# Attention and a gated feed-forward layer in one kernel: weight sums moved into the last pair of chunks, other banks, another static order

## The chip, the cores and the metric

The kernel runs on one core of a Trainium2 chip. The metric is the device time of one launch in microseconds, the median of the runs shown. Matrix products run on TensorE (PE), elementwise work on VectorE (DVE), ScalarE (ACT) and GpSimd (POOL); nearly all transfers are issued by SyncE (SP).

## The reference

```python
# attention: batch 8, heads 8, 576 tokens, head size 64; causal
scores = matmul(q, k.T) / 8
mask_local   = (rel >= 0) & (rel < 32)                 # heads 0 to 3
mask_strided = (rel >= 0) & (pos_q % 32 == pos_k % 32) # heads 4 to 7
attn = softmax(where(mask, scores, -1e9))
x = matmul(attn, v)          # as [4608 tokens, 512]
# feed-forward
xn = x / sqrt(mean(x * x) + 1e-6) * rms_g
g = xn @ w_gate              # 512 -> 1536
out = (g * sigmoid(g) * (xn @ w_val)) @ w_out   # 1536 -> 512
```

## The kernel before

**Precision.** Every large product is made of three passes. An operand x is split into a rounded high half (a cast) and a low half (a subtraction), both in the format that PE streams at full rate, and high x high, low x high and high x low are added in PSUM. So each operand costs a cast and a subtraction on ACT, DVE or POOL, and each 128x512 block of a product is three matmuls.

**Tiling.** Attention is cut into 96 units (`wus`, L434): batch b, pair of heads p, part j of three. Heads 0 to 3 (p = 0, 1) work on bands of tokens, heads 4 to 7 (p = 2, 3) on residues. Each unit runs `step_s` (scores on PE into the PSUM tile `pair`, maximum, exponential, norm; the split of q and k is `split`, L499), `step_t` (transposes, on DVE for most units) and `step_o` (values on PE, copied into `raw`). The result is cut into 9 chunks of 512 tokens, three `raw` tiles in turn. Chunks 0 to 6 (`NCL` = 7) pass through the feed-forward part one by one, while the attention of later chunks is made beside them; chunks 7 and 8 are done together at the end.

**A chunk of the loop.** It has 12 slots u, one per 128 columns of the 1536. `slot_g` and `slot_v` make gate and value into the banks `g` and `v` (L952), DVE and ACT form the product h (tanh on ACT, the steps at L967 and L978), `slot_h` splits it and `slot_o` adds it into the four output banks `a0` to `a3` (L1006). The output weight of a slot comes from a ring of `RING` = 4 buffers (`or0` to `or3`), filled from DRAM by `stream`. `rms` makes the next chunk's root: squares summed over the head pairs (`square`), a total over the partitions on PE, a root on ACT, one reciprocal over 128x512 on DVE (L896) and four scalings of `raw` (L900).

**The last pair.** `pair_of_chunks` (L1106) treats chunks 7 and 8 and the weights of gate and value as matrices of two by two blocks, so that seven products do for eight: A11, S1, A12, S2, S4, S3, A22. For each u, `quad(u)` (L1272) makes the seven, each six matmuls (L1283), into three banks p, q, r, and combines them on ACT and DVE; even and odd u have different banks. Four of the seven read sums of weights. `transform_gv` makes them for each u in the main loop: `joined` (L1052) adds the halves of gate and value, `minus` (L1056) forms the differences, `finish_set` splits them (L1070, L1076) and stores them in DRAM (`twg`); the pair fetches them back, two sets at a time. The sums on the other side, of the chunks, are made at its start in the buffers `ssq` and `srt` (L1212), which also hold output blocks on their way to DRAM. A second layer (`oproduct`, L1426) makes the output in seven products again, from sums of the output weight that `transform_o` has put into DRAM.

**PSUM.** There are eight banks. `g` and `v` are tiles of their own; `b0` and `b1` are the halves of the tile `pair`, `a0` and `a1` of `acc01`, `a2` and `a3` of `acc23`. The quads use (`g`, `v`, `b0`) and (`b1`, `a0`, `a1`) in turn.

**What sets the order.** Each operation is recorded by `Plan.op` with an engine (or several to choose from), a cost, the keys that it reads and writes, and whether it needs the SBUF port that DVE and POOL are taken to share. `Plan.order` computes due times from the end backwards (`series`, `latest`) and lays out a static order for each engine (`forward`): among the operations that could start within a hold time, the one due first. Two sets of parameters, `PASS_A` and `PASS_B`, hold before and after the point `SWITCH`. The order is then fixed; each engine runs its list in turn and waits where an operand isn't there.

Of the kernel before, what the change touches and what calls it, by code (L numbers as in the profile page):

```python
# [10 lines left out]
F32 = mybir.dt.float32  # L11
# [12 lines left out]
P = 128  # L24
# [5 lines left out]
NX = 3  # L30
RING = 4
# [22 lines left out]
PRE = 13  # L54
CD = 1.0
CA = 1.0
CP = 1.0
LATC = 150.0
EAT = 2000.0
PM = 15  # L60
# [83 lines left out]
class Plan:  # L144
# [15 lines left out]
    def op(self, eng, cost, at, fn, reads=(), writes=(), bytes_=0, rel=0.0, lock=(), tab=None, port=False, chain=False, also=None):  # L160
        i = len(self.ops)
        deps = set()
# [22 lines left out]

    def order(self):
# [12 lines left out]
    def series(self, users, hold, chf, dmt, rounds):  # L199
# [3 lines left out]
        for i in range(n - 1, -1, -1):  # L203
            ways, _, nb, _, _, _, chain = ops[i]
            eng = min(ways, key=lambda e: ways[e][0])
            own = ways[eng][0] + (dmt if nb else self.TAIL[eng])
            t = max([-due[u] + (0.0 if eng in ops[u][0] else self.LAT) for u in users[i]], default=0.0) + own
# [8 lines left out]
    def latest(self, users, took, length):  # L216
# [7 lines left out]
        for _ in range(n):  # L224
# [12 lines left out]
            for d in ops[i][1]:  # L237
                t = start[i] + (0.0 if on[d] == e and not ops[d][2] else self.LAT) + long[d] - ops[d][0][on[d]][0]
# [6 lines left out]
    def forward(self, users, due, hold, due2=None, hold2=None):  # L245
# [6 lines left out]
        def enter(i):  # L252
            ways, deps, _, rel, _, _, _ = ops[i]
            ready[i] = {e: max([end[d] + (0.0 if on[d] == e and not ops[d][2] else self.LAT) for d in deps] + [rel]) for e in ways}
# [24 lines left out]
        while len(out) < n:  # L279
            best = None  # L280
            for e, lst in avail.items():
                cand = []
                for i in lst:
# [6 lines left out]
                    cand.append((s, due[i], i))  # L290
# [38 lines left out]
def attn_moe(ctx: ExitStack, tc: tile.TileContext, qT: bass.AP, kT: bass.AP, vl: bass.AP, vs: bass.AP,  # L329
# [57 lines left out]
    tt = [sbt([P, 2 * CH], n) for n in ("tt", "th0")]  # L387

# [45 lines left out]
    wus = [(b, p, j) for b in range(NB) for p in range(NH // 2) for j in range(3)]  # L434
# [5 lines left out]
    for i in range(n_pro - TLAG, last + 1):  # L440
# [43 lines left out]
    for u in range(RING):  # L484
        wraw["o", u] = sb.tile([P, 1024], U32, name=f"or{u}")

    def wkey(key):
        return ("or", key[1] % RING) if key[0] == "o" else ("w", key)

    def wtag(key):  # L490
        return f"or{key[1] % RING}" if key[0] == "o" else f"w{key[0]}{key[1]}"
# [254 lines left out]
    def step_o(units):  # L746
# [23 lines left out]
        for x, (i, vt, m, n, tl, pT, po) in enumerate(todo):  # L770
# [27 lines left out]
            def evac(e, moves=moves):  # L798
# [6 lines left out]
               writes=[("raw", c % NX, p) for c in cs] + ["free2"] * (i == 11), also=way("e", ("DVE", dve(nt * m) + 80 * (len(moves) - 1), False)))  # L805


    def square(c, p, at):
# [15 lines left out]
        else:  # L824
            dk = "srt" if p else "ssq"
# [7 lines left out]
            if p:  # L833
# [3 lines left out]
    def rms(c, bk, at):  # L837
# [58 lines left out]
        op("DVE", 3270, at, lambda: nc.vector.reciprocal(out=roots["srt"], in_=roots["srt"]), writes=["srt"])  # L896
# [100 lines left out]
    def slot_o(c, u, at):  # L997
        h = 0
        if c and u == 2 * (c - 1):
            transform_o(c - 1)  # L1000
        for t in (0, 2, 1, 3):
            def fn(t=t):
                sl = slice(t * P, t * P + P)
                wt = W[("o", u)]
# [3 lines left out]
            op("PE", 681, at + t, fn, reads=[("hh", h), ("hl", h), wkey(("o", u))], writes=[("S", t // 2 + 1), ("T", t // 2 + 1), f"a{t}"] if u == 0 and c == 0 else [f"a{t}"], chain=True)  # L1008
# [20 lines left out]
    twg = [dp.tile([P, 2048], F32, name=f"tg{u}") for u in range(NU)]  # L1029
# [3 lines left out]
    def tset(i, w):  # L1033
        if (i, w) not in TS:
            TS[i, w] = sb.tile([P, 2 * CH], F32R, name=f"{'tl' if w else 'th'}{i}")
        return TS[i, w]

    def tkeys_of(i):
        return [("ts", i, w) for w in range(2)]
# [11 lines left out]
    def joined(key, dst, dk):  # L1051
        elementwise(CH, lambda e: both(e).tensor_tensor(out=dst, in0=W[key][:, 0].bitcast(F32), in1=W[key][:, 1].bitcast(F32), op=ALU.add),  # L1052
                    [wkey(key)], [dk])

    def minus(width, dst, a, b, keys):
        elementwise(width, lambda e: both(e).tensor_tensor(out=dst, in0=a, in1=b, op=ALU.subtract), [], keys)  # L1056

    turn_ = [0]

    def finish_set(dram, dk):  # L1060
        i = 0
        more = [("zo", 0), ("zo", 1)] if not turn_[0] else []
# [687 lines left out]
```

## Time and profile before

| | |
|---|---|
| time, median of 3 runs | 1041.87 us (1041.74 to 1043.63) |
| the profiled execution's own time | 1042.75 us |
| its span, first to last instruction | 1041.0 us |
| granted PE clock, mean | 0.990 |
| DMA traffic | 146.28 MB, mean 141 GB/s |

The page divides the span into 40 slices; a digit is the busy share in tenths:

```profile
PE   8899998999999999999999999999999989999998
...
DVE  4799999988789887887889998889996775455781
...
POOL 6224656763367653765236633356533510001300
PEclk9899999999999999999999999999999989999999
```

Attention and loading fill the first part, the main loop runs to about 840 us (slice 32), the pair of chunks from there to the end. POOL has almost nothing to do in the last eight slices. A row of a group of instructions gives line, engine, operation, result and operands, shape and count, then the busy time and the mean of one, then the engine's idle time ahead of them and who ended it.

### The profile page before, as it was taken

The numbers are of one execution on the slowest core, as the hardware profiler recorded it, in microseconds if no ns is written. First come the engines' busy times: TensorE is split into PE (matmuls) and PEld (weight loads), VectorE is DVE, ScalarE is ACT, GpSimd is POOL, SyncE is SP. The second block draws the span as 40 slices with busy tenths as digits, with TensorE's granted clock in tenths as the row PEclk, the third lists the DMA queues.
The fourth block names the chain that finished last, engine by engine and source line by source line (L and its number), as shares of the span: only waits on it lengthen the run. The fifth ranks groups of instructions, "written<-read, shape, count | busy, mean of one in ns | idle before, by whom it ended". The sixth has DMA issues, their size and how long they took to land. (4 is left out here: it accounts for less than half of the span.)

```text
span 1041.0 us, 15504 instructions
## 1 busy us (share of the span) xinstructions
PE 1001.9 (96%) x5104; PEld 806.6 (77%) x5104; DVE 831.7 (80%) x1677; ACT 577.5 (55%) x1520; POOL 444.9 (43%) x416
## 2 busy tenths in 40 slices
PE   8899998999999999999999999999999989999998
PEld 6677776778887888878887778887788867767776
DVE  4799999988789887887889998889996775455781
ACT  7899967555564546645645555556654443233430
POOL 6224656763367653765236633356533510001300
PEclk9899999999999999999999999999999989999999
DMA  9884343553245433334333534324441123433542
GB/s 305 279 312 179 117 136 129 172 192 98 82 137 161 143 132 125 137 117 155 124 97 96 175 103 142 111 90 149 163 137 53 61 102 106 166 132 122 172 139 74
DMA packets 59472, 146.28 MB, mean 141 GB/s; under 512 B 6080, under 2 KB 22016, under 8 KB 59392
## 3 DMA queue, kind: packets, MB, share of 16 engines
q1 hardware_dynamic: 58624, 144.45, 41.2%
q10 hardware_dynamic: 768, 0.85, 0.3%
q8 instruction: 40, 0.66, 0.2%
q14 instruction: 40, 0.33, 0.1%
HBM read 110.68 MB, written 34.60 MB: 140 GB/s over the span
## 5 line engine op out<-in xcount | busy, mean ns | idle before, releaser
L952 PE MATMUL g<-xh,wg 128*128 128x512 f32 x672 | 212.5, 398 | 4.3 <-DVE e L967 4.2
L1006 PE MATMUL acc<-or,hh 128*128 128x512 f32 x672 | 209.4, 392 | 0.9 <-POOL or L1575 0.5
L952 PE MATMUL v<-xh,wv 128*128 128x512 f32 x664 | 208.1, 395 | 0.0
L994 POOL TENSOR_TENSOR hl<-e,hh 128x512 fp32r<-128x512 f32 x84 | 113.4, 1350 | 142.5 <-ACT hh L985 133.8
L677 ACT ACTIVATE pp<-pp,mx 96x128 f32<-96x128 f32 (+2 forms) x296 | 114.0, 387 | 105.4 <-DVE mx L665 96.2
L686 POOL TENSOR_TENSOR pp<-pp,mx 96x512 f32<-96x512 f32 (+3 forms) x87 | 92.4, 1062 | 151.3 <-DVE mx L683 114.6
L1006 PEld LDWEIGHTS acc<-or,hh 128*128 128x128 f32 x672 | 125.4, 188 | 28.6 <-POOL or L1575 0.9
L952 PEld LDWEIGHTS g<-xh,wg 128*128 128x128 f32 x672 | 122.4, 190 | 30.3 <-DVE e L967 6.5
L952 PEld LDWEIGHTS v<-xh,wv 128*128 128x128 f32 x664 | 121.8, 188 | 26.4 <-DVE e L978 0.9
L952 PE MATMUL g<-xl,wg 128*128 128x512 f32 x336 | 131.5, 391 | 1.7 <-DVE xl L928 1.7
L1006 PE MATMUL acc<-or,hl 128*128 128x512 f32 x336 | 131.1, 390 | 0.0
L952 PE MATMUL v<-xl,wv 128*128 128x512 f32 x332 | 129.7, 391 | 0.0
L729 DVE STREAM_TRANSPOSE pT<-pp 32x128 f32<-32x128 f32 (+1 forms) x375 | 109.8, 293 | 14.0 <-POOL pp L686 8.2
L529 DVE TENSOR_TENSOR qk<-xx,qk 64x576 fp32r<-64x576 f32 x92 | 96.4, 1048 | 2.7
L985 ACT CAST hh<-e 128x512 fp32r<-128x512 f32 x84 | 52.0, 619 | 79.0 <-PE acc L1006 72.4
L524 ACT CAST qk<-xx 64x576 fp32r<-64x576 f32 x138 | 88.5, 671 | 7.6 <-PE pair L622 5.9
L965 ACT ACTIVATE e<-g 128x512 f32<-128x512 f32 x84 | 49.8, 593 | 65.0 <-PE g L952 63.0
L967 DVE SCALAR_TENSOR_TENSOR e<-e,g 128x512 f32<-128x512 f32 x84 | 57.2, 681 | 26.1 <-ACT e L965 24.7
L952 PEld LDWEIGHTS g<-xl,wg 128*128 128x128 f32 x336 | 63.7, 189 | 15.8 <-DVE xl L928 2.1
L1006 PEld LDWEIGHTS acc<-or,hl 128*128 128x128 f32 x336 | 63.2, 188 | 13.5
L952 PEld LDWEIGHTS v<-xl,wv 128*128 128x128 f32 x332 | 62.5, 188 | 13.5
L978 DVE SCALAR_TENSOR_TENSOR e<-e,v 128x512 f32<-128x512 f32 x83 | 56.8, 684 | 11.4 <-PE v L952 7.7
(453 smaller groups left out, 1818.0 us busy)
## 6 DMA issues: line engine op xcount, KB each, us to landing
or<-wos SPq DMA_DIRECT2D x72, 512.0 KB, 3.3
xx<-in_qT_dram SPq DMA_DIRECT2D x26, 288.0 KB, 2.9
xx<-in_kT_dram SPq DMA_DIRECT2D x25, 288.0 KB, 4.1
vt<-in_vl_dram SPq DMA_DIRECT2D x16, 384.0 KB, 4.1
wg<-in_wgv_dram SPq DMA_DIRECT2D x12, 512.0 KB, 8.1
wv<-in_wgv_dram SPq DMA_DIRECT2D x12, 512.0 KB, 7.9
or<-in_wo_dram SPq DMA_DIRECT2D x12, 512.0 KB, 4.1
wos<-or SPq DMA_DIRECT2D x12, 512.0 KB, 3.2
```

The lines of the kernel that those rows point to most:

```text
L524: nc.scalar.copy(out=d, in_=s)
L529: (nc.gpsimd if eng == "Pool" else nc.vector).tensor_tensor(out=d, in0=s, in1=y.bitcast(F32), op=ALU.subtract)
L677: nc.scalar.activation(out=pv[:, h, x], in_=sp[h][:, x] if i < PM else pv[:, h, x], func=AF.Exp, scale=0.125 if i < PM else 1.0, bias=mx[: ...
L686: (nc.vector if e == "DVE" else nc.gpsimd).tensor_tensor(out=pv, in0=pv, in1=mx.unsqueeze(3).broadcast_to([m, 2, nt, n]), op=ALU.mult)
L729: nc.vector.transpose(out=dst[32 * y:32 * y + 32, :, 32 * x:32 * x + 32], in_=src[32 * x:32 * x + 32, :, 32 * y:32 * y + 32])
L952: nc.tensor.matmul(out=out, lhsT=wt[:, w, sl], rhs=xhl[x, kc], start=(kc == 0 and i == 0), stop=(kc == KC - 1 and i == 2))
L965: op("ACT", act(CH, True), at + MO, lambda: nc.scalar.activation(out=e, in_=bank["g"], func=AF.Tanh, scale=0.5), reads=["g"], writes=[ek], ...
L967: op("DVE", dve(CH), at + MO, lambda: nc.vector.scalar_tensor_tensor(out=e, in0=e, scalar=1.0, in1=bank["g"], op0=ALU.add, op1=ALU.mult), ...
L978: op("DVE", dve(CH), at + MO, lambda: nc.vector.scalar_tensor_tensor(out=e, in0=e, scalar=0.5, in1=bank_of(c, ("v", u))[0], op0=ALU.mult, ...
L985: nc.scalar.copy(out=hh[h], in_=e)
L994: (nc.vector if n == "DVE" or h else nc.gpsimd).tensor_tensor(out=hl[h], in0=e, in1=hh[h].bitcast(F32), op=ALU.subtract)
L1006: nc.tensor.matmul(out=acc[t], lhsT=x[h][:, sl], rhs=wt[:, w], start=(u == 0 and i == 0), stop=(u == NU - 1 and i == 2))
```

## The change

1. **Weight sums of gate and value.** Two of the twelve are made in the last chunk of the loop (u = 1 and 5), the others inside the pair, each some quads ahead of its use; they stay in SBUF, in three sets (`th0`/`tl0`, `th1`/`tl1`, `or0`/`or1`), and no longer go through DRAM. They work in two pairs of temporaries in turn (`tt` and `xx0`/`xx1`).
2. **Sums of the output weight.** Still through DRAM; five stand where they stood, that of (6, 10) moves to (1, 10). The ring of the output weight has five buffers, its keys count over chunks.
3. **Banks and order of the quads.** Even u: p = `g`, q = `a0`, r = `b0`; odd u: `v`, `a1`, `b1`. The planner's keys are the tiles, not the banks. S3's result is combined into the temporary `s5`, not into bank q, and the last step of a quad multiplies two SBUF operands on DVE or POOL. The products are recorded as 1, 2, 5, 6, 3, 7 for u = 0 and 1 together, then 4 of u = 0, and then for each u the order 5, 6, 2, 3, 7, the next u's 1, 4 (1: A11, 2: A12, 3: S4, 4: A22, 5: S1, 6: S2, 7: S3).
4. **The last batch** does its head pairs in the order 2, 3, 0, 1, the values of its last four units come in twos, and chunk 7's squares of the band heads follow their first part.
5. **Last root and sums.** The last chunk's root has its own operations (`last_root`) in `xx0`, `xx1`, `pp0`, `pp1`; the sums of the chunks are made in `xx0` and `xx1`. X of A22 and of S3 lie in other buffers.
6. **Reciprocals** of 128x512 become four of 128x128.
7. **Second layer.** Its banks are (`g`, `v`), (`a0`, `a2`), (`b0`, `a1`) instead of (`a2`, `v`), (`a3`, `b0`), (`g`, `b1`); the last chunk of the loop fills its output banks in the order 0, 1, 2, 3.
8. **Planner.** Other values of `PASS_A`, `PASS_B`, `SWITCH`; from chunk 2 on, operations of the loop other than the large products are preferred by 60 us (feed-forward) or 30 us (attention) over their due time. The other new constants are zero.

```diff
-RING = 4
+RING = 5
+BA = 30000.0
+BM = 60000.0
+CB = 2
-PASS_A = ([300.0, 50.0, 300.0, 100.0], 0.0, 4000.0, 6)
-PASS_B = ([37.5, 400.0, 200.0, 200.0], 0.1, 4000.0, 7)
-SWITCH = 140000.0
+PASS_A = ([25.0, 0.0, 150.0, 50.0], 0.2, 8000.0, 12)
+PASS_B = ([25.0, 600.0, 300.0, 400.0], 0.2, 12000.0, 5)
+SWITCH = 220000.0
...
+        self.lift.append(0.0 if chain else self.boost)
...
-                    cand.append((s, due[i], i))
+                    cand.append((s, due[i] - self.lift[i], i))
...
+    tile_of = {"g": "g", "v": "v", "b0": "PR", "b1": "PR", "a0": "A01", "a1": "A01", "a2": "A23", "a3": "A23"}
...
-    wus = [(b, p, j) for b in range(NB) for p in range(NH // 2) for j in range(3)]
+    wus = [(b, p, j) for b in range(NB) for p in ((2, 3, 0, 1) if b == NB - 1 else range(NH // 2)) for j in range(3)]
...
-            d = s + (PG - 1 - (i - PP0) % PG) + PVL
+            d = s + (PG - 1 - (i - PP0) % PG if i < last - 3 else (last - i) % 2) + PVL
...
-        op("DVE", 3270, at, lambda: nc.vector.reciprocal(out=roots["srt"], in_=roots["srt"]), writes=["srt"])
+        for q in range(0, CH, P):
+            op("DVE", 890, at, lambda q=q: nc.vector.reciprocal(out=roots["srt"][:, q:q + P], in_=roots["srt"][:, q:q + P]), writes=["srt"])
...
-        if c and u == 2 * (c - 1):
-            transform_o(c - 1)
+        if (c, u) in ((1, 0), (1, 10), (2, 2), (3, 4), (4, 6), (5, 8)):
+            b = plan.boost
+            plan.boost = 0.0
+            transform_o(u // 2, c)
+            plan.boost = b
...
+    def last_root():
+        c = NCH - 1
+        rt, ri = raw[c % NX], c % NX
+        s0, s1, k0, k1 = (lambda: x32(0)), (lambda: x32(1)), ("xx", 0), ("xx", 1)
...
+    def transform_gv(u, z=0):
+        a, b, ka, kb = temps_of(z)
+        left, right = (lambda t: lambda: t()[:, LH]), (lambda t: lambda: t()[:, RH])
+        joined(("g", u), a, ka)
+        joined(("v", u), b, kb)
+        minus(CH, a, b, a, [ka, kb])
+        minus(256, left(b), right(b), left(b), [kb])
+        minus(256, right(b), right(b), left(a), [kb, ka])
+        minus(256, right(a), left(a), right(a), [ka])
+        finish_set(u % NS, z)
+    NS = 3
...
-        f = ["ssq", "srt"]
+        f, fk = (lambda: x32(0), lambda: x32(1)), (("xx", 0), ("xx", 1))
...
         def bank_keys(n):
-            if n in seen:
-                return [n]
-            seen.add(n)
-            return [n] + ([("S", 0), ("T", 0)] if n[0] == "b" else [])
+            t = tile_of[n]
+            if t in seen or len(t) == 1:
+                return [t]
+            seen.add(t)
+            return [t] + ([("S", 0), ("T", 0), "b0", "b1"] if t == "PR" else ["a0", "a1"] if t == "A01" else ["a2", "a3"])
...
-            p, q, r = (("g", "v", "b0"), ("b1", "a0", "a1"))[z]
+            p, q, r = (("g", "a0", "b0"), ("v", "a1", "b1"))[z]
...
-                out=banks[q], in0=banks[p], scalar=0.5, in1=temp(s5), op0=ALU.mult, op1=ALU.add), reads=[tk[s5], p], writes=[q])
+                        out=temp(s5), in0=banks[p], scalar=0.5, in1=temp(s5), op0=ALU.mult, op1=ALU.add), reads=bank_keys(p), writes=[tk[s5]])
...
-            value(1, t2, q)
+                    elementwise(CH, lambda e: both(e).tensor_tensor(out=htile(u, 1), in0=temp(t2), in1=temp(s5), op=ALU.mult),
+                                [tk[t2], tk[s5]], htake(u, 1))
...
-        for u in range(NU):
-            if u == 0:
-                for i in range(NS):
-                    fetch_set(i)
-            quad(u)
-            if u + NS < NU:
-                fetch_set(u + NS)
+        transform_gv(2, 0)
+        steps = [quad(u) for u in range(NU)]
+        for m in "125637":
+            for u in range(2):
+                steps[u][0](m, False)
+            for u in range(2):
+                steps[u][1](m)
+        steps[0][0]("4")
+        for u in range(1, NU):
+            if u > 1:
+                steps[u][0]("56237")
+            if u + 1 < NU:
+                steps[u + 1][0]("1")
+            steps[u][0]("4")
+            for v in [3, 4] if u == 1 else [u + 3] if u + 3 < NU else []:
+                transform_gv(v, v % 2)
...
-        P2, Q2, R2 = ("a2", "v"), ("a3", "b0"), ("g", "b1")
+        P2, Q2, R2 = ("g", "v"), ("a0", "a2"), ("b0", "a1")
...
-            if c and u % 6 == 3:
-                transform_gv(2 * (c - 1) + u // 6)
+            plan.boost = 0.0
+            if c == NCL - 1 and u in (1, 5):
+                transform_gv(u // 5)
```

More of the change, by code (lines that the diff above doesn't have):

```diff
@@ L253, in enter @@
             ways, deps, _, rel, _, _, _ = ops[i]
-            ready[i] = {e: max([end[d] + (0.0 if on[d] == e and not ops[d][2] else self.LAT) for d in deps] + [rel]) for e in ways}
+            ready[i] = {e: max([end[d] + (0.0 if on[d] == e and not ops[d][2] else self.lat(i)) for d in deps] + [rel]) for e in ways}
             for e in ways:
@@ L824, in square @@
         else:
-            dk = "srt" if p else "ssq"
+            lead = p == (0 if c < NB - 1 else 2)
+            dk = "ssq" if lead else "srt"
             def sq(e):
@@ L1092, in transform_o @@
[L1092 to L1101 removed]
+               reads=tkeys_of(i, w), writes=[(dk, w)], bytes_=P * 4096)
@@ new lines, in quad, with step @@
+            args = {"1": ("A11", p, basic("g", 0), gk, True, False), "5": ("S1", r, trans(1), tkw, True, False),
+                    "6": ("S2", p, trans(2), tkw, False, False), "2": ("A12", q, basic("g", 256), gk, True, True),
+                    "3": ("S4", r, basic("v", 256), vk, False, True), "7": ("S3", p, trans(3), tkw, False, False),
+                    "4": ("A22", p, trans(4), tkw, False, True)}
+            def step(ms, follow=True):
+                for m in ms:
+                    product(*args[m])
+                    if follow:
+                        after(m)
```

275 lines of the change are left out of this document (158 added, 117 removed), and 2 rows, old and new, of the table xplace.

## The prediction

> **What bounds the kernel now.** I read the busy times first.
>
> ```profile
> span 1041.0 us, 15504 instructions
> ...
> PE 1001.9 (96%) x5104; PEld 806.6 (77%) x5104; DVE 831.7 (80%) x1677; ACT 577.5 (55%) x1520; POOL 444.9 (43%) x416
> ```
>
> TensorE (PE) is the bound, and the change leaves the number of large matmuls alone, so a gain can only come from time in which PE does not stream. The 96% hides some of that: a matmul is booked until its modelled end while its successor has long started. So I count matmuls by stretch instead (the chain of waits gives the pitch, the windows give the counts in brackets behind PE's busy time).
>
> ```profile
> 861.41 1.36 PE g L1283 x6
> ...
> 839.50:857.20 17.70, 13.15 (x44) 9.59 (x44) 14.88 (x23) 7.49 (x12) 1.29 (x1) 0.81 0.16 61
> 857.20:980.00 122.80, 115.30 (x481) 88.71 (x481) 68.87 (x104) 42.18 (x74) 12.98 (x11) 1.00 0.41 136
> ...
> 1000.00:1025.00 25.00, 24.75 (x108) 19.92 (x107) 12.42 (x23) 2.97 (x5) 0.00 (x0) 1.00 0.24 79
> ```
>
> Six matmuls take 1.36 us, 0.227 each. A dense stretch (108 in 25 us, 24.5 us of pitch) loses 0.5 us. The start of the pair of chunks holds 44 matmuls, 10.0 us of pitch, in 17.7: **7.7 us lost**. The rest of its first layer holds 481, 109.0 us, in 122.8: **13.8 us lost**. The start is one chain:
>
> ```profile
> 847.94 0.33 SPq L1025 DMA_DIRECT2D out_dram<-ssq  x1
> ...
> 850.06 0.69 DVE L1212 TENSOR_TENSOR ssq<-raw 128x512 f32<-128x512 f32 x1 [1.90 <-DMA out_dram<-ssq]
> ...
> 850.79 0.62 ACT L1181 CAST qk<-ssq 128x512 fp32r<-128x512 f32 x1 [2.38 <-DVE ssq L1212]
> ...
> 851.46 0.79 PE L1283 MATMUL pair<-qk,th 128*128 128x512 f32 x1 [4.22 <-ACT qk L1181]
> ```
>
> `ssq` still holds an output block that is being stored, so the sum for S1 waits for that store and PE stands 4.22 us; then the clock is low (0.81 over this stretch: 0.19 x 17.7 = 3.4 us of it). In the quads the loss repeats:
>
> ```profile
> 891.19 3.04 PE pair L1283 x12
> ...
> 912.69 3.04 PE pair L1283 x12
> ...
> 906.47 0.70 DVE L1303 TENSOR_TENSOR acc<-acc,pT 128x512 f32<-128x512 f32 x1 [1.32 <-ACT hh L1297]
> ...
> 907.20 0.60 ACT L1310 ACTIVATE hl<-acc 128x512 f32<-128x512 f32 x1 [0.77 <-DVE acc L1303]
> ...
> 907.85 0.73 PE L1283 MATMUL acc<-xh,wv 128*128 128x512 f32 x2 [0.67 <-ACT hl L1310]
> ```
>
> Two quads, 14 products, take 21.50 us where 14 x 1.36 = 19.04 would do. The last row is the tell: S4 writes `a1`, the tanh before it reads `a0`, and yet S4 waits for it. The two banks are halves of one tile, `acc01`; waits go by tile, and the planner of before tracks banks, so it put S4 where it must stall.
>
> In the main loop PE waits rarely (waits of PE from 160 to 825 us: total, times, longest):
>
> ```profile
> PE pair L622 <- DVE qk L529: 5.6, 5, 2.4
> PE g L952 <- DVE e L967: 3.6, 2, 1.9
> PE g L858 <- DVE e L967: 1.8, 2, 1.4
> PE g L952 <- DVE xl L928: 1.7, 1, 1.7
> PE pair L622 <- ACT th L1070: 1.3, 1, 1.3
> ```
>
> 14.0 us in all. The longest, in order of time, and the two windows with a low clock:
>
> ```profile
> 327.75 7.25 DVE L529 TENSOR_TENSOR qk<-xx,qk 64x576 fp32r<-64x576 f32 x4
> ...
> 329.20 1.69 POOL L1052 TENSOR_TENSOR tt<-wv 128x512 f32<-128x512 f32 x1
> 330.85 1.80 POOL L1052 TENSOR_TENSOR tt<-wg 128x512 f32<-128x512 f32 x1
> ...
> 335.15 0.98 PE L622 MATMUL pair<-qk 128*126 128x256 f32 x3 [2.40 <-DVE qk L529]
> ...
> 325.00:350.00 25.00, 22.60 (x123) 18.46 (x122) 20.26 (x41) 12.48 (x36) 17.77 (x17) 0.93 0.37 122
> 725.00:750.00 25.00, 23.13 (x101) 18.54 (x100) 23.78 (x42) 15.50 (x42) 14.50 (x14) 0.93 0.43 150
> ```
>
> Four DVE subtractions take 7.25 us, 1.81 each, while POOL makes a weight sum (L1052); PE's scores wait for them. Each low window costs 0.07 x 25 = 1.7 us more.
>
> **The change part by part.** Durations of single instructions (min/median/max ns where three numbers stand together; else us in all and mean ns):
>
> ```profile
> L1052 POOL TENSOR_TENSOR tt<-wg x12: 1277/1295/1797, 184.5 to 726.0; 128x512 f32<-128x512 f32 x12
> ...
> L1056 POOL TENSOR_TENSOR tt<-tt x68: 724/739/1805, 161.2 to 822.5; 128x256 f32<-128x256 f32 x59, 128x512 f32<-128x512 f32 x9
> ...
> L1076 POOL TENSOR_TENSOR tl<-tt,th x26: 1274/1293/1824, 180.9 to 757.5; 128x512 fp32r<-128x512 f32 x26
> ...
> L1076 DVE TENSOR_TENSOR tl<-tt,th x10: 676/692/1670, 360.2 to 830.5; 128x512 fp32r<-128x512 f32 x10
> ...
> L529 DVE TENSOR_TENSOR qk<-xx,qk x92: 730/755/2739, 176.8 to 775.7; 64x576 fp32r<-64x576 f32 x92
> ...
> L967 DVE SCALAR_TENSOR_TENSOR e<-e,g x84: 627/686/690, 51.7 to 836.3; 128x512 f32<-128x512 f32 x84
> ...
> L1297 ACT ACTIVATE pT<-pair 128x512 f32<-128x512 f32 x12 | 7.2, 600 | 18.6 <-PE pair L1283 16.3 <-DVE pT L1314 2.3
> ...
> L896 DVE RECIPROCAL srt<-srt x8: 3343/3354/3354, 154.0 to 838.3; 128x512 f32<-128x512 f32 x8
> ...
> L952 PE MATMUL v<-xl,wv 128*128 128x512 f32 x332 | 129.7, 391 | 0.0
> ```
>
> *Own buffers for the sums, new opening order.* The sums go to `xx0`, `xx1`, which the last attention step has left, so the 1.90 us wait for the store goes. What is late next is the normalisation of the last chunk, on the same engine just ahead of the sums, and the X halves. Behind it the opening is now A11, A11, A12, A12: four products, 5.4 us, that need no sum, where before one of them stood right ahead of S1. With no gap of 4.22 us the low clock goes too. Bounds: 0.4 us left (the dense rate) to 7.7 (nothing won); I take 1.2, nearer the dense rate since 5.4 us of cover stand against a wait of 4.22. **Gain 6.5.** The last batch done strided heads first and in groups of two lets chunk 7 finish earlier; it adds no instruction and I give it nothing more.
>
> *Banks by tile.* Quads use (`g`,`a0`,`b0`) and (`v`,`a1`,`b1`), the planner tracks tiles, and the order is 5 6 2 3 7, the next quad's 1, then 4. Distances by the rows: a product is 1.36. From 3 to the next quad's 5 (both in `pair`) lie three products, 4.1 us, for a merge and a value, about 2.2. From 2 to the next 2 (`acc01`) lie six, 8.2 us, for merge, tanh, gate: 0.7 + 0.6 + 0.7. The tightest is 7 to 4 on one bank: one product, 1.36, against the modelled tail of a matmul (0.39 - 0.23), one DVE step of 0.69 and the hand-over between engines, some 0.9: 0.45 us of slack, if DVE is free. So the tile waits should go; what DVE does in between decides. Bounds: 2.5 left (0.5 per 25 us) to 13.8; I take 5, towards the dense row, because one step of seven is tight. **Gain 8.8.**
>
> *Weight sums inside the pair.* Ten of twelve leave the loop up to 825 us (two stay in its last chunk), 24 stores and 24 fetches of 512 KB and their SP issues go; DMA is busy 0.41 there, so I count that as nothing. Each sum is five steps of 512 and three of 256: on POOL 5 x 1.29 + 3 x 0.74 = **8.7 us**, on DVE half, plus two ACT casts of 0.6. They now stand beside PE's 9.52 us a quad (7 x 1.36). POOL is nearly empty there (12.98 of 122.8) and has room; DVE had 68.87 of 122.8. Three buffers let a set be made two quads ahead, 19 us, so it is hidden: cost 0; without the cover see the rivals. In the loop POOL loses ten times 8.7 us. Three waits above had a weight sum of gate or value on POOL at that moment, the one at 335 us and these two:
>
> ```profile
> 201.63 1.67 POOL L1052 TENSOR_TENSOR tt<-wg 128x512 f32<-128x512 f32 x1
> ...
> 203.98 0.63 PE L622 MATMUL pair<-qk 128*126 128x256 f32 x3 [1.28 <-DVE qk L529]
> ...
> 725.95 1.63 POOL L1052 TENSOR_TENSOR tt<-wg 128x512 f32<-128x512 f32 x1
> ...
> 729.38 0.73 PE L952 MATMUL g<-xh,wg 128*128 128x512 f32 x2 [1.87 <-DVE e L967]
> ```
>
> 1.3 + 2.4 + 1.9 and the two clocks are 9.0 us. All could go, none could, and a new static order makes collisions of its own. **Gain 3**, a third, as the loop's waits come from several causes.
>
> The Trainium skill, "TensorE: Matmul & The Clock Gate" (HAM oscillation), asks for an idle time above about 3.4 us before the clock halves. The trace differs: 0.93 stands in the window of a gap of 2.40. By the page those two clocks would not belong to the gaps, the loop's term would be 5.6 / 3 = 1.9, and the forecast 1.1 later; the rows decide.
>
> *Reciprocal in four.* 3.35 us on DVE becomes four pieces; bounds 0 to 0.3 more for each of eight chunks, off PE's path, and the gate step L967 can pass between: I count 0. *Ring of five, output sums spread differently* (one of six moves from chunk 6 to chunk 1): same instructions, more room; 0. *Last layer:* its first product now writes `g`, `v`, the second freed only after the last quad's tanh and gate, 1.3 us; six half products on `g`, 4.1 us, cover it. Without cover 1.3.
>
> Sum: 6.5 + 8.8 + 3 = 18.3 us. The profiled execution took 1042.75 us, 0.88 above the median of the runs shown; 1042.75 - 18.3 - 0.88 = **1023.6**.
>
> **The rivals.**
>
> *Sums late (slower).* Rows for it: L1052 and L1076 reach 1.8 us when DVE reads SBUF too. Five steps of 1.8 and three of about 1.05 are 12.2 us, more than a quad. Nine quads (3 to 11) at 12.2 instead of 10.67 (9.52 + 13.8/12), three at 9.7: +11 us; the other gains, 9.5, nearly pay for it: 1043. But nine gaps of 2.7 us are longer than the 2.40 that lowered the clock, 1.7 us each: up to 1058. I take 1050. It decides from a set time of about 11.5 us. Against it: medians are 1.29 and two temporaries and DVE can share the work.
>
> *DVE behind POOL.* The quad's last step now multiplies two SBUF operands, as L529 does, and the row at 327.75 shows what POOL makes of such a step: 1.81 for 0.755. DVE works in order, so the step between 7 and 4 comes up to 1.3 us late against 0.45 of slack: 0.9 x 12 = 10.8 us, 1034. The Trainium skill, "SBUF — State Buffer" (Who interferes with whom), says this as a rule: a VectorE step with two SBUF inputs and a GpSimd step that reads SBUF exclude each other. By that rule the trace agrees, 7.25 us for four. Against: steps with a PSUM operand are untouched (L967 never takes over 690 ns, and POOL is busy 43% of the span).
>
> *It doesn't do what it says.* The normalisation is as late as the store was: the start's 6.5 stays lost, and if the loop gives back 9 us (half of the 14.0 and 3.4 that this order loses), 1039 or, with the tight step failing too, 1047.
>
> **How the numbers follow.** A measurement of this kernel tells 0.2%, 2.1 us, from no change. Forecast, 1016 to 1031: 0.46. Loop and quads gain nearly all, 1010 to 1016: 0.08. DVE behind POOL or the start not won, 1031 to 1039.8: 0.19. Within 0.2%: 0.07. Sums late, around 1050: 0.13. Loop loses more than the pair wins, around 1046: 0.07. Faster 0.73, same 0.07, slower 0.20. The range 1010 to 1047 leaves out about 0.11 above and 0.04 below.
>
> **What would show it.** The stretch from the first L1283 product to the second layer should shrink from 140.5 us to about 125, with over 105 matmuls in each 25 us and no low clock at its start. Two quads should repeat in under 20 us. A PE wait on a cast of the weight set (th, tl or their new place) would mean sums late; one on the step between 7 and 4, DVE behind POOL. In the loop, L529 should come below its mean of 1048 ns:
>
> ```profile
> L529 DVE TENSOR_TENSOR qk<-xx,qk 64x576 fp32r<-64x576 f32 x92 | 96.4, 1048 | 2.7
> ```
>
> Wrong above all if PE waits between 50 and 825 us grow by more than 15 us.

## The result and the profile after

The changed kernel takes **1015.79 us**, median of four executions (1014.29 to 1017.39); before, run beside it, takes 1042.75 (1041.74 to 1045.89). The ratio is 0.9737, interval 0.9709 to 0.9764: faster by 2.6%, some 27 us, where 18.3 were forecast. The execution that was profiled took 1014.29 us, the fastest of the four, so the two traces differ by 28.5 us.

The head of the page after, and its group of the subtractions at L529, now L545 (busy time, mean ns of one, idle ahead):

```profile
span 1012.5 us, 15391 instructions
...
PE 992.7 (98%) x5104; PEld 805.4 (80%) x5104; DVE 846.3 (84%) x1745; ACT 572.1 (57%) x1502; POOL 416.6 (41%) x390
...
L545 DVE TENSOR_TENSOR qk<-xx,qk 64x576 fp32r<-64x576 f32 x92 | 83.0, 902 | 6.3 <-ACT qk L540 3.8
```

PE's busy time hardly moves (1001.9 to 992.7) while the span falls by 28.5: as in the prediction, the gain has to be read by stretches and counts. The windows of after: the loop up to 10 us ahead of the pair, the pair's start as long as in the prediction (17.7 us), and the rest of its first layer. The columns are window, length, then busy time and count of PE, weight loads, DVE, ACT and POOL, granted clock, DMA share and GB/s:

```profile
160.00:821.70 661.70, 655.49 (x3371) 537.21 (x3370) 561.51 (x1222) 368.33 (x994) 279.68 (x259) 1.00 0.33 108
...
831.50:849.20 17.70, 17.54 (x77) 14.32 (x77) 15.72 (x27) 8.70 (x16) 1.52 (x1) 1.00 0.16 60
849.20:951.50 102.30, 102.30 (x446) 83.31 (x445) 85.65 (x126) 42.97 (x74) 59.24 (x46) 1.00 0.17 56
```

and the same windows of before that were not shown yet (the loop to 10 us ahead of its pair, the 28 us from there, and 80 us among the quads):

```profile
160.00:829.60 669.60, 654.65 (x3357) 536.14 (x3356) 568.20 (x1189) 374.54 (x1021) 345.71 (x315) 0.99 0.38 127
829.60:857.60 28.00, 23.45 (x89) 17.80 (x88) 22.59 (x31) 12.17 (x19) 6.12 (x5) 0.88 0.27 96
859.60:939.60 80.00, 75.67 (x318) 58.43 (x318) 42.20 (x65) 24.07 (x42) 2.57 (x2) 1.00 0.40 135
```

At 0.227 us a matmul, 77 are 17.5 us of the start's 17.7, and 446 are 101.1 of 102.3. Where the 28.5 us come from:

| | before | after | gain | forecast |
|---|---|---|---|---|
| up to the pair's first product | 839.5 us | 831.5 us | 8.0 | 3 |
| start of the pair, time without matmuls | 7.7 of 17.7 | 0.2 of 17.7 | 7.5 | 6.5 |
| rest of its first layer, the same | 13.8 of 122.8 | 1.2 of 102.3 | 12.6 | 8.8 |
| from there to the end | 61.0 | 61.0 | 0 | 0 |

(The two middle rows add up to 20.1 and the layer shrinks by 20.5: the windows of before hold two more matmuls.) In the loop PE's idle time falls from 669.60 - 654.65 = 14.95 us to 6.21, and where before has two stretches with a low clock, at 335 and 731 us, after has one, at 168 us, 1.7 us less: 10.4 together. After is some ten matmuls, 2.3 us, behind when the loop's window opens at 160 us, which leaves the 8.0. What PE still waits for most there (waits of PE, 160 to 825 us: total, times, longest); its waits for the subtractions were 5.6 us in before:

```profile
PE g L970 <- DVE e L985: 4.4, 4, 2.6
PE pair L638 <- DVE qk L545: 0.9, 2, 0.5
```

The start, in order of time (start, duration, engine, line, operation; the second fence is pieces of the chain of waits):

```profile
813.29 1.29 POOL L1296 TENSOR_TENSOR xx<-raw 128x512 f32<-128x512 f32 x1 [1.29 <-DVE raw L1118]
...
819.33 0.68 DVE L1296 TENSOR_TENSOR xx<-raw 128x512 f32<-128x512 f32 x1
...
838.16 0.34 SPq L1046 DMA_DIRECT2D out_dram<-ssq  x1
```

```profile
814.61 3.48 DVE raw L1118 x2
...
831.02 0.61 DVE e L985
...
831.67 1.67 PE g L1356 x6
```

The two sums of chunks that S1 needs start on POOL at 813.29 and on DVE at 819.33 us; the later one stands 12 us ahead of the first product and 19 us ahead of the first store of an output block from `ssq`, the buffer that they no longer use. The scalings of the last chunk by its root that they need (L1118) are done at 818.1 us. From there the chain stays almost wholly on DVE up to the gate step of the loop's last slot (L985), which releases the first product: DVE has no slack there. Two quads on the chain, from an A11 on `v` to the A11 two quads later:

```profile
862.29 1.40 PE v L1356 x6
...
867.83 1.40 PE acc L1356 x6
...
877.51 1.40 PE acc L1356 x6
...
881.65 1.40 PE v L1356 x6
```

881.65 - 862.29 = 19.36 us for 14 products; 19.04 would be without any loss, 21.50 was before. `acc01`, whose halves were banks q and r of one odd quad, now gets one product per quad, 9.7 us apart.

### The profile page after: what moved, and what is told of

Read it like the earlier page. It is cut to its first block, busy times and chain, and to the rows that moved or that the text cites. A ratio compares the mean times of both kernels' runs of the same rounds, so it can differ in the third digit from the quotient of the medians.

```text
span 1012.5 us, 15391 instructions
## 1 busy us (share of the span) xinstructions
PE 992.7 (98%) x5104; PEld 805.4 (80%) x5104; DVE 846.3 (84%) x1745; ACT 572.1 (57%) x1502; POOL 416.6 (41%) x390
## 4 chain that ended last, share of the span: by engine, by line
PE 81%; DVE 12%; ACT 4%; issue 2%; DMA 1%; DVEq 0%; ACTq 0%
PE g L970 18%; PE v L970 18%; PE acc L1027 18%; PE g L1356 3%; PE pair L1356 3%; PE v L1356 3%; PE pair L782 3%; PE pair L638 3%; DVE qk L545 2%; PE acc L1356 2%; PE g L1521 2%; PE v L1521 2%; PE acc L1521 2%; DVE raw L918 1%; DVE pT L745 1%
## 5 line engine op out<-in xcount | busy, mean ns | idle before, releaser
L702 POOL TENSOR_TENSOR pp<-pp,mx 96x512 f32<-96x512 f32 (+3 forms) x87 | 88.3, 1017 | 156.4 <-DVE mx L699 106.3
L545 DVE TENSOR_TENSOR qk<-xx,qk 64x576 fp32r<-64x576 f32 x92 | 83.0, 902 | 6.3 <-ACT qk L540 3.8
L985 DVE SCALAR_TENSOR_TENSOR e<-e,g 128x512 f32<-128x512 f32 x84 | 57.4, 683 | 27.4 <-ACT e L983 26.5
L970 PEld LDWEIGHTS v<-xl,wv 128*128 128x128 f32 x332 | 62.5, 188 | 13.4
```

The costliest lines, as they stand in the source:

```text
L545: (nc.gpsimd if eng == "Pool" else nc.vector).tensor_tensor(out=d, in0=s, in1=y.bitcast(F32), op=ALU.subtract)
L702: (nc.vector if e == "DVE" else nc.gpsimd).tensor_tensor(out=pv, in0=pv, in1=mx.unsqueeze(3).broadcast_to([m, 2, nt, n]), op=ALU.mult)
L970: nc.tensor.matmul(out=out, lhsT=wt[:, w, sl], rhs=xhl[x, kc], start=(kc == 0 and i == 0), stop=(kc == KC - 1 and i == 2))
L985: op("DVE", dve(CH), at + MO, lambda: nc.vector.scalar_tensor_tensor(out=e, in0=e, scalar=1.0, in1=bank["g"], op0=ALU.add, op1=ALU.mult), ...
```

## The experiments

Each is one edit of the kernel before (names with b_) or of the changed kernel (a_); times are medians, and ratios go to before on the same chip. Every edit makes the planner lay out the order anew, so a time alone says little: the reading is by stretch. **Loop idle** is the window from 160 us to 10 us ahead of the pair's first product, less PE's busy time in it; **start** is the matmuls in the 28 us that follow (123 when dense), **quads** those in the 80 us from 20 us behind the first product (353 when dense). By the rows above before has 14.95 us, 89 and 318. After has 6.21 us by its row, and for the other two the rows below. A stretch that an edit doesn't touch can move as well: a_nos5, an edit of the quads, has 10.74 us of loop idle where after has 6.21, while b_s5 and b_tilekeys, edits of the pair in before, have 15.31 and 14.44 against 14.95.

```profile
821.70:849.70 28.00, 27.43 (x118) 21.69 (x117) 25.41 (x39) 11.56 (x20) 6.40 (x4) 1.00 0.10 38
851.70:931.70 80.00, 80.00 (x349) 65.11 (x348) 68.78 (x101) 32.47 (x57) 51.49 (x40) 1.00 0.12 40
```

### Where the loop's gain comes from

**b_onesum**: before, with one sum of the twelve made and fetched for all quads.

```diff
-in_=twg[u][:, 1024 * w:1024 * w + 1024]
+in_=twg[0][:, 1024 * w:1024 * w + 1024]
...
-        if c and u % 6 == 3:
-            transform_gv(2 * (c - 1) + u // 6)
+        if c == 1 and u == 3:
+            transform_gv(0)
```

> The kernel before, leaving out eleven of the twelve weight sums of gate and value (all quads fetch the first one's), so POOL and DVE have ten sums less in the loop, as after the change. If these sums make the loop's waits: 5 to 9 us less, 1033 to 1038. If the loop's waits come from the order as such: 1041 to 1044.

1031.78 us, ratio 0.9879 (0.9857 to 0.9900). Its loop window:

```profile
160.00:816.40 656.40, 649.68 (x3356) 533.94 (x3356) 537.27 (x1155) 366.47 (x1009) 270.69 (x247) 1.00 0.34 111
```

In this window POOL is 75 us less busy than in before and DVE 31 us, and loop idle falls from 14.95 to 6.72 us; start (89) and quads (318) stay as they were. PE's waits at 335 us (2.40), at 447 us (1.30, for a cast of a weight set, th L1070) and at 606 us (1.38) are gone, those at 204 and 729 us fall from 1.28 to 0.30 and from 1.87 to 0.67, and neither low clock is left. So the sums cost the loop some 8 us of idle time, and 3.4 us of low clock with it, not the 3 of the forecast. Their stores, 22 of 24, go as well; the waits named are for steps on DVE and ACT, none for a DMA.

**a_sumsloop**: after, with all twelve sums back in the loop and through DRAM.

```diff
-        finish_set(u % NS, z)
+        finish_set(0, z, twg[u], ("twg", u))
...
-                transform_gv(v, v % 2)
+                fetch_set(v)
...
-            if c == NCL - 1 and u in (1, 5):
-                transform_gv(u // 5)
+            if c and u % 6 == 3:
+                transform_gv(2 * (c - 1) + u // 6)
```

> The changed kernel, but all twelve weight sums of gate and value are made in the main loop where they stood and go through DRAM into the three sets. If taking them out of the loop gave the loop's gain, PE waits on DVE come back there: 1020 to 1026 us. If the loop's gain came from the order alone: 1014 to 1018. If the sums cost something inside the pair, this is faster than the changed kernel.

1023.95 us, ratio 0.9816 (0.9800 to 0.9833):

```profile
160.00:829.00 669.00, 656.83 (x3373) 536.09 (x3372) 572.10 (x1231) 378.34 (x1019) 356.06 (x324) 1.00 0.39 129
...
859.00:939.00 80.00, 80.00 (x349) 65.11 (x348) 43.91 (x67) 27.71 (x47) 11.14 (x8) 1.00 0.48 158
```

Loop idle doubles, to 12.17 us, and the quads stay dense at 349. The move of the sums is worth 6 us of the loop's idle time here, and neither harms nor helps the quads.

**b_planafter** and **a_planbefore**: the planner's parameters alone, put into before, and taken back in after.

```diff
-PASS_A = ([300.0, 50.0, 300.0, 100.0], 0.0, 4000.0, 6)
-PASS_B = ([37.5, 400.0, 200.0, 200.0], 0.1, 4000.0, 7)
-SWITCH = 140000.0
+PASS_A = ([25.0, 0.0, 150.0, 50.0], 0.2, 8000.0, 12)
+PASS_B = ([25.0, 600.0, 300.0, 400.0], 0.2, 12000.0, 5)
+SWITCH = 220000.0
```

(a_planbefore has the reverse, and `BA` and `BM` at zero.)

> The kernel before with the changed kernel's PASS_A, PASS_B and SWITCH (its preference of the loop's operations isn't there). If the structure makes the gain: 1038 to 1046. If the parameters do a good part alone: 1034 or less.

> The changed kernel with the planner's parameters of before (PASS_A, PASS_B, SWITCH, no preference). If the structure makes the gain: at most 4 us more, 1016 to 1020. If the static order's parameters make the loop's gain: 9 us or more, from 1025 on.

b_planafter: 1034.96 us, ratio 0.9915 (0.9894 to 0.9936). Its loop window and its group of subtractions:

```profile
160.00:821.90 661.90, 653.87 (x3368) 536.80 (x3366) 553.51 (x1204) 377.20 (x1012) 340.00 (x313) 1.00 0.38 128
```

```profile
L529 DVE TENSOR_TENSOR qk<-xx,qk 64x576 fp32r<-64x576 f32 x92 | 81.3, 884 | 2.7
```

POOL still makes all sums (340.00 us), and yet loop idle is 8.03 us and a subtraction takes 884 ns in the mean where 1048 stood: another order keeps the same work apart better. a_planbefore: 1020.04 us, ratio 0.9774 (0.9757 to 0.9791):

```profile
160.00:825.90 665.90, 659.86 (x3390) 541.33 (x3389) 546.92 (x1199) 371.06 (x1020) 269.34 (x246) 1.00 0.33 107
825.90:853.90 28.00, 24.89 (x98) 18.70 (x97) 27.74 (x39) 13.33 (x24) 12.09 (x9) 0.94 0.11 39
855.90:935.90 80.00, 79.60 (x342) 63.32 (x341) 76.56 (x113) 29.06 (x51) 44.62 (x39) 1.00 0.13 40
```

Loop idle is 6.04 us with the old parameters too; what it loses against after is at the start (98) and in the quads (342). So in before taking the sums out (8.2 us) and planning around them (6.9) win most of the same loop idle, and the two don't add up: 15 us is all there was, and about 6 are left with both. The parameters are no sure cure, though: a_sumsloop has them too, beside the other changes, and with the sums in the loop it keeps 12.17 us.

### The start

**b_ownbuf**: before, with the sums of chunks in `xx0` and `xx1`.

```diff
-        f = ["ssq", "srt"]
+        f = ["xx0", "xx1"]
+        own = [("xx0", None), ("xx1", None)]
...
-                        [rk[1][k], rk[1][2 + k]], [tk[f[k]]])
+                        [rk[1][k], rk[1][2 + k]], claim(own[k]))
```

> The kernel before, with the sums of the chunks made in xx0 and xx1 and not in the buffers of the output blocks. If the wait for the store is the start's loss, its 7.7 us shrink to 3 or less: 1036 to 1039 us, no half clock behind it. If the normalisation of the last chunk is as late: less than 2 us gained, 1041 to 1044.

1040.57 us, ratio 0.9973 (0.9956 to 0.9990), though the start is filled: 122 matmuls. Ahead of it stand 13.4 us with 45 (the windows, then the timeline, with the idle time ahead of an instruction and who ended it in brackets):

```profile
160.00:835.40 675.40, 657.93 (x3365) 537.27 (x3364) 573.08 (x1200) 373.90 (x1015) 353.43 (x318) 0.99 0.38 125
...
822.00:835.40 13.40, 11.69 (x45) 8.99 (x44) 10.48 (x12) 6.14 (x11) 9.32 (x7) 0.87 0.00 1
835.40:863.40 28.00, 28.00 (x122) 22.42 (x121) 25.50 (x37) 15.57 (x25) 6.05 (x4) 1.00 0.32 113
```

```profile
826.75 0.73 PE L952 MATMUL g<-xh,wg 128*128 128x512 f32 x2 [1.71 <-DVE e L967]
```

The buffers do at the start what the forecast said: (122 - 89) x 0.227 = 7.5 us. But this order loses 2.5 us more in the loop, and a gap of 1.71 us with a low clock behind it now stands 19 us ahead of the first product, where in before the gap of 4.22 stood inside the pair. PE is also ten matmuls, 2.3 us, behind at 160 us (929 against 939), and the quads hold 314. So the start's gain hardly shows in the time. Nor do the new buffers fill the start in every order: a_planbefore and a_oldbanks, which have them, hold 98 and 103, with one wait of some 2.1 us each, for the loop's last product h and for an output block that is still in its bank, and a low clock.

### The quads

Six kernels ask which part makes the quads dense. **a_bankkeys**: after, with the planner tracking banks again.

```diff
-            t = tile_of[n]
-            if t in seen or len(t) == 1:
-                return [t]
-            seen.add(t)
-            return [t] + ([("S", 0), ("T", 0), "b0", "b1"] if t == "PR" else ["a0", "a1"] if t == "A01" else ["a2", "a3"])
+            if n in seen:
+                return [n]
+            seen.add(n)
+            return [n] + ([("S", 0), ("T", 0)] if n[0] == "b" else [])
```

> The changed kernel, but the planner's keys in the pair are banks again, not tiles; banks, buffers and sums stay new. If the planner's knowledge of tiles took the quads' loss away, the quads stall again, about 1 us each: 1026 to 1029 us, matmuls per 25 us in the quads near 100. If the new banks and the recorded order did it, within 2 us of the changed kernel: 1014 to 1018, 110 per 25 us.

**b_tilekeys**: before, with the keys of the banks in the pair replaced by those of their tiles.

```diff
+        tile_of = {"b0": "PR", "b1": "PR", "a0": "A01", "a1": "A01", "a2": "A23", "a3": "A23"}
...
+        def op(*a, reads=(), writes=(), **k):
+            writes = tiles_for(writes)
+            plan.op(*a, reads=tiles_for(reads), writes=writes, **k)
```

> The kernel before, with nothing changed but the planner's keys in the pair: tiles, not banks. If the knowledge of tiles is enough, the loss of 13.8 us in the quads falls to 5 or less: 1030 to 1035 us. If it needs the new banks or the new recorded order: 1040 to 1044.

**a_oldbanks**: after, with the banks of before.

```diff
-            p, q, r = (("g", "a0", "b0"), ("v", "a1", "b1"))[z]
+            p, q, r = (("g", "v", "b0"), ("b1", "a0", "a1"))[z]
```

> The changed kernel with the banks of before in the quads (g, v, b0 and b1, a0, a1), planned with tile keys. If the knowledge of tiles is what counts, the planner finds an order that PE doesn't wait in: at most 3 us more than the changed kernel, 1016 to 1019. If dealing the banks out by tiles counts, the quads stall by 0.8 us or more each: 1025 or more.

**a_nos5** and **b_s5**: S3 combined into bank q again in after; into the temporary, with two SBUF operands in the last step, in before (the reverse of this diff).

```diff
-                        out=temp(s5), in0=banks[p], scalar=0.5, in1=temp(s5), op0=ALU.mult, op1=ALU.add), reads=bank_keys(p), writes=[tk[s5]])
+                        out=banks[q], in0=banks[p], scalar=0.5, in1=temp(s5), op0=ALU.mult, op1=ALU.add), reads=[tk[s5]] + bank_keys(p), writes=bank_keys(q))
...
-                    elementwise(CH, lambda e: both(e).tensor_tensor(out=htile(u, 1), in0=temp(t2), in1=temp(s5), op=ALU.mult),
-                                [tk[t2], tk[s5]], htake(u, 1))
+                    value(1, t2, q)
```

> The changed kernel, with S3's result combined into bank q again and the quad's last step reading that bank. If holding q to the end of a quad was what made PE wait in the quads (neither the planner's keys nor the banks did), they lose 5 us or more again where the changed kernel loses 1.1: 1020 us or more. If the recorded order removed the loss: 1014 to 1018.

> The kernel before, with S3's result combined into the temporary s5 and the quad's last step multiplying two SBUF operands. If that frees the banks that PE waits for, the quads' loss falls from 13.4 to 7 us or less: 1035 to 1038. If it needs the recorded order: 1040 to 1045. If DVE is then held up by POOL there, the quads lose more than 13.4.

**a_recorder**: after, with the products recorded quad by quad.

```diff
-        for m in "125637":
...
-        for u in range(1, NU):
...
-            steps[u][0]("4")
+        for u in range(NU):
+            steps[u][0]("1526374")
```

> The changed kernel, with the products recorded quad by quad as before (1, 5, 2, 6, 3, 7, 4, without the next quad's first product ahead of the last). If the recorded order removed the quads' loss or the start's: 5 us or more back in the pair, 1020 us or more. If the temporary s5 did: 1014 to 1018.

| | time, us | ratio (interval) | start | quads |
|---|---|---|---|---|
| a_bankkeys | 1021.06 | 0.9780 (0.9762 to 0.9798) | 115 | 349 |
| a_oldbanks | 1019.31 | 0.9774 (0.9751 to 0.9797) | 103 | 347 |
| a_nos5 | 1023.92 | 0.9825 (0.9806 to 0.9844) | 115 | 345 |
| a_recorder | 1018.62 | 0.9774 (0.9755 to 0.9793) | 117 | 349 |
| b_tilekeys | 1039.02 | 0.9961 (0.9941 to 0.9981) | 84 | 322 |
| b_s5 | 1040.35 | 0.9969 (0.9956 to 0.9982) | 104 | 318 |

The row behind "quads" of a_bankkeys, then that of b_tilekeys:

```profile
857.80:937.80 80.00, 80.00 (x349) 65.11 (x348) 68.27 (x92) 32.08 (x56) 47.89 (x43) 1.00 0.13 40
```

```profile
860.10:940.10 80.00, 75.56 (x322) 59.52 (x321) 43.31 (x64) 25.47 (x43) 5.40 (x5) 1.00 0.39 132
```

By its time a_nos5 reaches the 1020 us at which its expectation blames the quads, and a_bankkeys, a_oldbanks and a_recorder lie between their two ranges. The counts acquit the quads: what a_nos5 loses is mostly loop idle, and the other three are 13 or 14 matmuls behind after already at 160 us (last section).

The planner's knowledge of tiles is neither needed (349 without it) nor enough (322 with it alone). The temporary is neither needed (345 without) nor enough (318 with it alone). The new banks and the recorded order aren't needed either (347 and 349 without); whether one of them would be enough in before wasn't tried. PE's order isn't the same in the dense kernels. What can be read from the traces is the distance in it: in before, A12 and S4 of odd quads lie on the two halves of `acc01` with one product between them; in a_oldbanks they lie on the same halves with five or six between, and PE waits 0.2 us in all from 860 to 975 us. In the same stretch of before the recorded waits are 6.2 us, these two the largest (total, times, longest):

```profile
PE acc L1283 <- ACT hl L1310: 2.0, 3, 0.7
PE pair L1283 <- DVE acc L1334: 1.7, 3, 0.8
```

The first is the wait of S4 for A12's tanh. The second, of A22 for the step that combines S3, belongs to the same crowd: A12's gate reads `a0`, starts only when S4 on `a1` has ended, and DVE then has four steps to do ahead of A22. In b_tilekeys the wait on `acc01` for the tanh is gone, but S4 of even quads stands directly behind S1 on one bank, `b0`, and PE waits there for the copy of S1's result (timeline):

```profile
900.08 0.73 PE L1302 MATMUL pair<-xh,wv 128*128 128x512 f32 x2 [0.69 <-ACT pT L1316]
```

No single part taken out of after brings the stall back, and none of the parts that were put into before removes it (b_planafter has 313, b_ownbuf 314). Which of them suffice, alone or together, stays open, and that distance is the cause is a reading of the traces, not tested by itself.

### Reciprocal and last batch

**a_batch_recip**: after, with the last batch in its old order and one reciprocal of 128x512, the two edits that the prediction counted at nothing.

```diff
-    wus = [(b, p, j) for b in range(NB) for p in ((2, 3, 0, 1) if b == NB - 1 else range(NH // 2)) for j in range(3)]
+    wus = [(b, p, j) for b in range(NB) for p in range(NH // 2) for j in range(3)]
...
-            lead = p == (0 if c < NB - 1 else 2)
+            lead = p == 0
...
-        for q in range(0, CH, P):
-            op("DVE", 890, at, lambda q=q: nc.vector.reciprocal(out=roots["srt"][:, q:q + P], in_=roots["srt"][:, q:q + P]), writes=["srt"])
+        op("DVE", 3270, at, lambda: nc.vector.reciprocal(out=roots["srt"], in_=roots["srt"]), writes=["srt"])
```

> The changed kernel, with the last batch in its old order and one reciprocal of 128x512. If neither counts: 1014 to 1018. If the order of the last batch gives the pair its ready start, 3 us or more come back ahead of the first sums; if the reciprocal's length holds up DVE, PE waits on the gate step (L967 of before) at each root: 1019 or more either way.

1023.03 us, ratio 0.9815 (0.9795 to 0.9834) against 0.9737 (0.9709 to 0.9764) for after: some 7 or 8 us. Start (119) and quads (349) are those of after, so they go in the loop and ahead of it: loop idle is 9.79 us against 6.21, a second low clock stands in the loop, at 287 us (1.7 us), and by 160 us 916 matmuls are done against 929 (2.9 us). A piece of its chain of waits, and what PE does behind it (timeline):

```profile
278.06 3.35 DVE srt L913
```

```profile
282.79 0.72 PE L638 MATMUL pair<-qk 128*96 128x256 f32 x4 [0.71 <-DVE pp L680]
285.70 0.73 PE L969 MATMUL g<-xh,wg 128*128 128x512 f32 x2 [2.19 <-DVE mx L699]
287.79 0.79 PE L969 MATMUL g<-xl,wg 128*128 128x512 f32 x1 [1.36 <-DVE xl L945]
```

Behind this whole reciprocal PE stands 0.71 + 2.19 + 1.36 = 4.3 us, far from the last batch; behind the same root in after it stands 1.00 + 0.64 = 1.6 us, so the difference is 2.7 us and the low clock. Another 1.42 us come at 808 us, where the total for the last chunk's root waits for ACT.

But the pieces are on after's chain too: those of the root at 157 us,

```profile
158.39 1.73 DVE srt L914 x2
```

with 0.86 us each at 157.38 and 160.89, and one more of 0.85 us at 278.85. And in before, whose chain isn't followed back beyond 843 us, DVE works without a pause from a whole reciprocal to the gate step that PE waits for 1.87 us at 729 us (timeline),

```profile
719.26 3.35 DVE L896 RECIPROCAL srt<-srt 128x512 f32<-128x512 f32 x1
...
728.66 0.67 DVE L967 SCALAR_TENSOR_TENSOR e<-e,g 128x512 f32<-128x512 f32 x1
```

and likewise from 154.01 us to the wait of 1.78 us at 165. So a reciprocal costs what the order around it makes of it, in all three kernels. How much the last batch adds wasn't separated.

## Why the prediction was right, and where it was not

Direction and most mechanisms held; the time (1023.6 forecast, 1015.8 measured) came out lower, as the sum was 18.3 for 27 us, and the sizes were off one by one. The measured time lies just inside the stretch from 1010 to 1016, "loop and quads gain nearly all", which had a chance of 0.08; that is also what happened.

- **Start: right, though not by the cover.** 6.5 forecast, 7.5 found; "nothing won" was the far bound, and b_ownbuf shows that in the order of before the buffers alone fill the start. The four products that need no sum didn't come first: PE begins with A11, A11 and S1 (834.57 us), so only 2.9 us of cover stand ahead of S1. It wasn't needed, as both sums were made by 820.0 us. What was to be late next, the normalisation (L1118), ends 13.6 us ahead of the first product.
- **Quads: gain mis-sized, reason wrong.** 8.8 forecast, 12.6 found. The working left 5 us for the one tight step, 7 to 4 on one bank; it took none that PE felt: 1.2 us are lost in 102.3. And the reason put first, that the planner of before "tracks banks", was not what decided: a_bankkeys tracks banks and is as dense, and b_tilekeys tracks tiles and stalls elsewhere. The new order of products and banks did what its distances promised; which part of it was needed stays open.
- **Loop: mis-sized.** 3 forecast, 10.4 found in the loop's window and 8.0 up to the pair. The step that failed is the third taken of 9.0 us, because "a new static order makes collisions of its own". In b_onesum the three waits and both low clocks shrink by some 8 of these 9 us. A fourth wait, the 1.3 us for th L1070, goes with them; it is for a cast of a weight set, so it had to do with the sums as well, and the prediction left it out of the 9.0. b_planafter shows that an order alone can win much of it too; a_sumsloop shows that not every order does.
- **Weight sums in the pair at 0: right.** No wait of PE on a cast or difference of a weight set shows in the first layer; with the sums back in the loop (a_sumsloop) the quads are the same 349. *Sums late* did not come.
- **DVE behind POOL: the collision is there, the price is not.** The quad's last step takes up to 1.76 us beside a sum on POOL (timeline of after, DVE and then POOL):

```profile
853.27 1.76 DVE L1413 TENSOR_TENSOR raw<-pp,pT 128x512 f32<-128x512 f32 x1
```

```profile
853.20 1.29 POOL L1072 TENSOR_TENSOR xx<-wg 128x512 f32<-128x512 f32 x1
```

The shared port of the Trainium skill, "SBUF — State Buffer" (Who interferes with whom), agrees with 1.76 us for a step that takes 0.69 when free. The rival's next link failed: nothing on DVE that PE needs was late. The step between 7 and 4 (L1408) keeps its time, 675 to 692 ns, and nobody is recorded as waiting for it. The static order has the long steps where there is slack.
- **Reciprocal and last batch at 0: too low.** Together 7 or 8 us in after's surroundings, some 4 of it (2.7 and a low clock) behind one whole reciprocal. "Off PE's path" didn't hold even in before: two of its waits, 1.78 and 1.87 us, stand behind one. The second is among those that the prediction put down to a weight sum on POOL; in b_onesum, with whole reciprocals but without that sum, 0.67 us of it are left.
- **The clock.** As forecast, it isn't low at the start; the two low windows of the loop are gone, and a new one stands at 168 us (last section).

Single edits of after cost 4 to 9 us by their ratios although start and quads hardly move in some. In a_bankkeys, a_oldbanks and a_recorder some 3 us of that lie ahead of the loop, where their order is that of after (last section), so their ratios are not prices of the parts.

## What to carry to other kernels

Where an order is laid out by a planner, price a removed load by all waits that it stood beside, casts on another engine included, and don't add up two cures for the same waits. For a stall on a buffer shared by two results, look at the distance between them in the order that came out; no single one of the parts that change it (banks, keys, temporary, recorded order) was needed here. "Off the critical path" holds for one order only: follow an in-order engine back from the step that is waited for. Splitting a long instruction cost next to nothing (24.1 us for 28 pieces of the reciprocal, 23.5 for seven whole ones), but a wait can stand behind the pieces too.

## What the runs showed of the hardware beside that

The clock fell behind gaps of PE far shorter than 3.4 us, and not behind all of one length. In after the remaining case (timeline; the granted clock from 150 to 175 us is 0.93):

```profile
167.67 0.90 PE L970 MATMUL g<-xh,wg 128*128 128x512 f32 x2 [2.59 <-DVE e L985]
```

In the same stretch of before, with a similar share of idle time, it is 1.00:

```profile
165.38 0.73 PE L952 MATMUL g<-xh,wg 128*128 128x512 f32 x2 [1.78 <-DVE e L967]
...
171.93 0.50 PE L952 MATMUL g<-xl,wg 128*128 128x512 f32 x1 [1.70 <-DVE xl L928]
```

A low clock stands behind gaps of 2.59 (after), 2.40 and 1.87 (before) and 1.71 us (b_ownbuf), and none behind 1.78 and 1.70; what decides between them isn't shown. The Trainium skill, "TensorE: Matmul & The Clock Gate" (HAM oscillation), names about 3.4 us; the rows decide.

The first 160 us differ between kernels that have the same order there on PE, DVE, ACT and POOL. After, and then a_recorder (the window, then the longest wait of PE in it):

```profile
0.00:160.00 160.00, 151.03 (x929) 117.20 (x930) 136.09 (x299) 134.55 (x389) 69.71 (x81) 0.98 0.65 222
```

```profile
PE pair L653 <- DMA qk<-in_kT_dram: 2.2, 1, 2.2
```

```profile
0.00:160.00 160.00, 149.60 (x915) 115.64 (x915) 133.38 (x293) 131.12 (x379) 65.89 (x78) 0.96 0.66 220
```

```profile
PE pair L653 <- DMA qk<-in_kT_dram: 3.7, 1, 3.7
```

Fourteen matmuls are 3.2 us of the 5.8 us by which these two executions differ (the medians differ by 2.8), and none of it comes from the quads that a_recorder edits. A load that lands 1.5 us later and a longer stretch of low clock (0.02 x 160 = 3.2 us) are what the records differ in; why stays open. It may belong to the execution and not to the kernel: the four executions of a_recorder itself run from 1017.35 us, at a mean clock of 0.995, to 1020.11, at 0.992.
